# A group of small matmuls sooner, a transpose tied behind a feed-forward unit, four visits per chunk for six

## The chip, the cores and the metric

One core of a Trainium2 chip. The metric is the device time of one execution in microseconds (us). TensorE (PE in the rows) does matrix products, with its weight loads listed as PEld; VectorE is DVE, ScalarE is ACT, GpSimd is POOL, and SP only issues transfers. `L489` is line 489 of the kernel before.

## The reference

A delta-rule linear attention over 4 batches, 8 heads, 768 tokens and 48 channels a head, followed by two feed-forward layers of width 2048 on the 3072 x 384 result.

```python
k_n = k / (np.linalg.norm(k, axis=-1, keepdims=True) + 1e-06)
for t in range(S):
    y[:, :, t] = np.einsum('bhd,bhde->bhe', q[:, :, t], state)
    v_old = np.einsum('bhde,bhd->bhe', state, kt)
    state = state + bt[:, :, :, None] * np.einsum('bhd,bhe->bhde', kt, vt - v_old)
...
h = x @ w_in                     # layer 1: g = 0 below -1, h above 1, (h+1)^2/4 between
x = g @ w_out
h = x @ w_in; r = np.maximum(h, 0.0); out = (r * r) @ w_out      # layer 2
```

## The kernel before

**Attention** runs in 24 chunks of 32 tokens. A chunk c has six small steps on TensorE, each 64 little instructions but the last (`chunk_steps`): `ks` (keys times state; VectorE subtracts it from the values, L416), `tr` (the inverted triangle times that; ScalarE copies it out), `qs` (queries times state), `ku` (the state's update; VectorE and ScalarE copy the state to `st`, L456 and L457), `pu` (added onto the tile of `qs`; ScalarE copies it out) and `xt` (three transposes that make the chunk an input of the first layer). All but `ku` write PSUM tiles of one tag, `att`, which has two buffers; so do the grams.

**Triangles.** Chunks are taken in six groups of four. `gram(c)` (L272) multiplies a chunk's keys with its keys and queries, and VectorE masks the product into `gp` (L284). When a group's four grams are there, `tri` inverts its triangles together: VectorE transposes `gp` into `gm` (`begin`, L325), a short chain on ScalarE, VectorE and GpSimd scales it, then 30 steps follow, each a multiply and an add on GpSimd (L370, L376), one after another on the tile `tx`; last, VectorE transposes `tx` back into `gp` (`end`, L380). The `tr` of the group's first chunk needs that.

**Feed-forward.** A unit x is `hidden` of one block of tokens and one of 16 slices f of the width (nine matmuls into `h`, one buffer; then ScalarE L514 and L515 read it, VectorE L516, ScalarE L517, VectorE L518), then `rest` (ScalarE L526, VectorE L527: the high and the low part of g), and the output product `out_` of unit x - 2 (nine matmuls into `acc`). Layer 1 has nine blocks of 256 or 384 tokens (`SIZES` in chunks), layer 2 eight of 384. The block after the running one gets its attention meanwhile.

**Order.** TensorE's order is written by hand. Unit x has two slots, 2x and 2x+1; for each x the order is hidden(x), the small groups of slot 2x, out_(x-2), those of slot 2x+1. The tables `exa` (small matmuls) and `exb` (other work) hold what goes into which slot; `at[c]` is the slot of a chunk's first step, `ready[c]` that of its gram. The other engines' order is made at build time by a planner: it walks time by its own estimates of durations and puts on an engine's queue what it holds to be ready, what was traced earlier first. The engine then takes its queue strictly in that order. `tc.issue_after(ins)` lays an edge: what is traced inside, on the engine of `ins`, is queued behind `ins`. `later` does so for the last unit's L514 (ScalarE) and L516 (VectorE).

Group 1 is inverted around the start of the loop and its `end1()` is traced before the loop, with no edge. For groups 2 to 5 `tri_put` puts the scaling and the steps into the slots from `ready` on (all steps within six slots, `PACE`) and `end` into slot `at` of the group's first chunk, with no edge. The keys and queries of a chunk are loaded once, into a ring of six (`load_kq`); the chunk six further on is loaded when `qs` is done.

Of the kernel before, what the change touches and what calls it, by code (L numbers as in the profile page):

```python
# [21 lines left out]
GROUPS = [4] * 6  # L22
# [3 lines left out]
def kernel(  # L26
# [38 lines left out]
    LENT = 28  # L65
    RG = 3
    RAW = 3
    WT, WL = 3, 4
    GB = 2
    MANY = 4  # L70
# [31 lines left out]
    def att(shape, name):  # L102
        tag = "att"
        if turn[0] is not None:
            tag = early[turn[0] % len(early)]
            turn[0] += 1
        return ps.tile(shape, F32, tag=tag, bufs=2 if tag == "att" else 1, name=name)
# [6 lines left out]
    kqt, kvt, gp, nt, xh, xl = {}, {}, {}, {}, {}, {}  # L114


    def load_kq(c, tag="kqt", bufs=6):
        if c >= NCH:
            return
        t = kqt[c] = ring.tile([P, B2, H, 2 * T], F32, tag=tag, bufs=bufs, name="kqt")  # L120
        for o in range(2):
            nc.sync.dma_start(
                t[64 * o:64 * o + D].rearrange("p b h x -> p (b h x)"), kq[c, D * o:D * (o + 1)]
            )

    def load_kv(c):
        if c >= NCH:
# [87 lines left out]
    w2r = {}  # L215

    def fetch_w2(f):
        w2r[f] = ring.tile([P, 2, DM], F32, tag="kqt", bufs=6, name="w2r")
        nc.sync.dma_start(w2r[f], w2f[f])

    def place_w2(f):
# [33 lines left out]
    def per_bh(f):  # L255
        for h in range(H):
            for b in range(B):
                f(b, h, slice(T * b, T * (b + 1)), slice(64 * (b % 2), 64 * (b % 2) + D))

    def gram(c, lo=0, hi=2, late=0):  # L260


        n, j = group_of[c]
        if j == 0 and lo == 0:
            gp[n] = ring.tile([P, 2, GC, H, T], F32, tag="gp", bufs=2, name="gp")
            if GROUPS[n] < GC:
                nc.gpsimd.memset(gp[n][:, 0, GROUPS[n]:], 0.0)
        g = att([P, H, hi - lo, T], "g")

        def one_(b, h, p, pd):  # L270
            x = kqt[c][pd, b // 2, h]
            nc.tensor.matmul(  # L272
                g[p, h].rearrange("p x i -> p (x i)"), x[:, 0:T], x[:, lo * T:hi * T],
                start=h == 0, stop=True, skip_group_check=True,
            )

        per_bh(one_)

        dst = gp[n][:, lo:hi, j].rearrange("p x h i -> p h x i")
        if late > 1:  # L280
            nc.scalar.copy(dst, g)

        def keep():
            nc.vector.tensor_mul(  # L284
                dst,
                dst if late > 1 else g,
                mask[:, lo:hi].rearrange("p (o x) i -> p o x i", o=1)
                .to_broadcast([P, H, hi - lo, T]),
            )

        if late:
            return keep
        keep()
# [97 lines left out]
    def chunk_steps(c):  # L391
# [38 lines left out]
        def qs():  # L430
            o = t["o"] = att([P, H, D], "yy")
            of_state(o, 1)
            if c >= HEADS:
                kqt.pop(c)
                load_kq(c + 6)

        def pu():
            o = t["o"]
# [38 lines left out]
            nc.vector.tensor_sub(xl[n][:, :, cols], o, xh[n].bitcast(F32)[:, :, cols])  # L477
            done()

        return [ks, tr, qs, pu, ku, xt] if c < HEADS else [ks, tr, qs, ku, pu, xt]  # L480


    x2 = dram.tile([P, KT, NCH * P], F32, name="x2", bufs=1)
# [118 lines left out]
    w1f = flow(w1s)  # L602
    w1f.reverse()

    PACE = 6
    SPREAD = 3
    behind = [nullcontext]

# [6 lines left out]
    with tc.manual_schedule():  # L615
        for c in range(GC):
            load_kq(c)
        nc.sync.dma_start(bet, beta)
        first1()
        load_kq(4)  # L620
        load_kq(5)
        for c in range(3):
            load_kv(c)
        nc.gpsimd.memset(zero, 0.0)
        nc.gpsimd.memset(one, 1.0)
        nc.gpsimd.memset(tiny, 1e-36)
        nc.gpsimd.memset(neg1, -1.0)
        nc.scalar.activation(st[:, 0, 0, 0:1], one, AF.Sqrt, bias=zero)
        nc.gpsimd.memset(mask, 1.0)
        nc.gpsimd.memset(tx, 0.0)  # L630
        for b in range(B):
            for o, op in enumerate((ALU.is_ge, ALU.is_gt)):
                m_ = mask[T * b:T * (b + 1), o]
                nc.gpsimd.affine_select(
                    m_, m_, pattern=[[1, T]], compare_op=op, fill=0.0,
                    base=0, channel_multiplier=-1,
                )
        make_identity(nc, ident)
        for c in range(GROUPS[0]):
            gram(c, 0, 1)  # L640
        begin, pre, steps, end = tri(0, [(V, 0, 3), (V, 3, 9), (G, 9, T)])
        begin()
        go(pre[:1])
        masks = [gram(0, 1, 2, late=2)]
        cross_gram(0, 1)
        go(pre[1:])
        more_w1()
        masks += [gram(c, 1, 2, late=2) for c in range(1, GROUPS[0])]
        for c in range(HEADS):
            load_kq(c + 6)  # L650
        late = masks[HEADS:]
        masks[HEADS:] = [gram(c, late=1) for c in range(GFIRST[1], GFIRST[2])]
        go(steps)
        for c in range(3):
            value(c)
        ins = end()
        go(masks)
        behind[0] = lambda: tc.issue_after(ins.ins)
    ENGINES = {mybir.EngineType.PE}
    with tc.manual_schedule(engines=ENGINES):  # L660
# [15 lines left out]
        begin()  # L676
        go(pre)
        go(t1)
        end1()
        turn[0] = None  # L680

        SL = 2 * NF
# [2 lines left out]
        def put(n, slot, *fs):  # L685
            for i, f in enumerate(fs):
                exb.setdefault(SL * n + slot + i, []).append(f)

        def later(*fs):

            def one_(f):
                with tc.issue_after(marks[0].ins), tc.issue_after(marks[1].ins):
                    f()

            return [lambda f=f: one_(f) for f in fs]

        def put_a(n, slot, f):
            exa.setdefault(SL * n + slot, []).append(f)

        at, ready, due = {}, {}, [GFIRST[2]]
        for n in range(1, NB):
            todo = []
            for c in range(FIRST[n], FIRST[n] + SIZES[n]):
                left = {0: 1, 1: 1, 2: 0, 3: 2}[c % GC]
                for i, s_ in enumerate(chunk_steps(c)):
                    todo.append(((at, c) if i == 0 else None, s_))
                    x = due[0]
                    if i + left > 5 and x < NCH:  # L710
                        left -= 1
                        due[0] += 1
                        todo.append(((ready, x), lambda x=x: gram(x)))
            for i, (mark, s_) in enumerate(todo):
                o = 0 if n > 1 else HEAD
                slot = SL * (n - 1) + o + i * (SL - o) // len(todo)
                if mark:
                    mark[0][mark[1]] = slot
                put_a(0, slot, s_)
        for c in range(3, NCH):  # L720
            put(0, max(0, at[c] - 5), lambda c=c: value(c))

        def tri_put(g, a, z):
            begin, pre, steps, end = tri(g, [(G, 0, T)])
            begin()
            for i, s_ in enumerate(pre):
                put(0, a + i // 3, s_)
            a += 4
            for i, s_ in enumerate(steps):
                put(0, a + i * min(z - a, PACE) // len(steps), s_)  # L730
            put(0, z, end)

        for g in range(2, NG):
            a, z = ready[GFIRST[g] + GROUPS[g] - 1], at[GFIRST[g]]
# [99 lines left out]
```

## Time and profile before

| | us |
|---|---|
| median of 3 runs (1101.43 to 1104.24) | 1101.67 |
| the profiled execution | 1103.17 |
| its span, first to last instruction | 1101.1 |
| TensorE busy in the span | 995.3 (90%) |
| VectorE / ScalarE / GpSimd busy | 609.3 / 506.4 / 293.1 |
| mean granted TensorE clock | 0.963 of full speed |

A row of the timeline gives the start, the duration, the engine, the line, the operation, what it writes and reads, the shapes and the count; in brackets stands how long the engine was idle before it and what ended the idle time. TensorE's ends are modelled and overlap the next start, so that the time of a group of matmuls is best taken from its start to the start of the next.

### The profile page before, as it was taken

To read this page: it belongs to the slowest core of one execution; us is meant where nothing else is said; L and a number is where in the kernel's file an instruction comes from. 1 tells how busy PE (TensorE), PEld (TensorE's weight loads), DVE (VectorE), ACT (ScalarE), POOL (GpSimd) and SP (SyncE) were. 2 spreads that over 40 slices of the span, in tenths; PEclk is the share of its full clock that TensorE was granted. 3 is DMA by queue.
4 is the path that set the end of the run, shared out by engine and by line. 5 is a ranking of instruction groups with operands and counts; after the bars stand their busy time and mean duration, and the time that the engine had idled before them with its cause. 6 is when DMAs were issued, how large, how long until landed. Compare 5 with 4: busy or idle time off the path is not lost.

```text
span 1101.1 us, 32911 instructions
## 1 busy us (share of the span) xinstructions
PE 995.3 (90%) x14312; PEld 952.0 (86%) x14312; DVE 609.3 (55%) x1187; ACT 506.4 (46%) x1068; POOL 293.1 (27%) x446
## 2 busy tenths in 40 slices
PE   4345799969997997999799999899999999999998
PEld 3335699969986997899699999899999999999998
DVE  4998566754764583557644467744434343434333
ACT  1065466535544653555455666433333333333332
POOL 3467600850391058007600022310101010101000
PEclk9966899989998999899899999999999999999999
DMA  8065145223331340231211122201001010000000
GB/s 235 33 209 165 35 131 158 82 80 88 89 103 52 96 132 30 81 118 31 74 31 52 32 87 87 72 1 44 22 23 43 1 43 1 22 1 22 1 22 22
DMA packets 33488, 72.99 MB, mean 66 GB/s; under 512 B 3904, under 2 KB 17728, under 8 KB 33344
## 3 DMA queue, kind: packets, MB, share of 16 engines
q1 hardware_dynamic: 33344, 70.89, 20.9%
q8 instruction: 112, 1.84, 0.7%
q14 instruction: 32, 0.26, 0.1%
HBM read 55.15 MB, written 15.73 MB: 64 GB/s over the span
## 4 chain that ended last, share of the span: by engine, by line
PE 64%; POOL 15%; DVE 11%; issue 4%; ACT 3%; DMA 1%; SPq 0%; DVEq 0%; POOLq 0%; ACTq 0%
PE h L489 29%; PE acc L489 29%; POOL tx L376 7%; POOL t L370 7%; DVE g L518 1%; PE g L272 1%; DVE t L370 1%; DVE tx L376 1%; DVE wl L161 1%; PE tr L420 1%; PE yy L406 1%; DVE wl L164 1%; PE ks L406 1%; PE yy L440 1%; PE sps L451 1%
## 5 line engine op out<-in xcount | busy, mean ns | idle before, releaser
L489 PE MATMUL h<-xh,w 128*128 128x384 f32 (+1 forms) x1632 | 325.8, 336 | 31.3 <-ACT g L515 28.2
L489 PEld LDWEIGHTS h<-xh,w 128*128 128x128 f32 x1632 | 276.7, 193 | 37.5 <-ACT g L515 27.8
L527 DVE TENSOR_TENSOR gl<-g,gh 128x384 fp32r<-128x384 f32 (+1 forms) x272 | 167.2, 615 | 133.3 <-ACT gh L526 128.5
L526 ACT CAST gh<-g 128x384 fp32r<-128x384 f32 (+1 forms) x272 | 134.5, 494 | 209.7 <-DVE g L518 107.8
L489 PE MATMUL h<-xl,w 128*128 128x384 f32 (+1 forms) x816 | 181.3, 331 | 0.0
L489 PE MATMUL acc<-gh,w 128*128 128x384 f32 (+1 forms) x864 | 170.3, 333 | 7.2 <-ACT gh L526 6.5
L521 DVE TENSOR_TENSOR g<-r 128x384 f32<-128x384 f32 x128 | 71.3, 557 | 157.7 <-ACT r L520 157.7
L489 PE MATMUL acc<-w,gh 128*128 128x384 f32 x768 | 155.6, 337 | 1.6 <-DVE e L534 1.6
L520 ACT ACTIVATE r<-h,zero 128x384 f32<-128x384 f32 x128 | 74.5, 582 | 166.4 <-PE h L489 166.4
L489 PEld LDWEIGHTS acc<-gh,w 128*128 128x128 f32 x864 | 139.1, 193 | 12.7 <-ACT gh L526 6.6
L489 PEld LDWEIGHTS h<-xl,w 128*128 128x128 f32 x816 | 143.4, 193 | 0.0
L489 PEld LDWEIGHTS acc<-w,gh 128*128 128x128 f32 x768 | 136.3, 188 | 1.9 <-ACT gh L526 1.9
L514 ACT ACTIVATE r<-h,one 128x384 f32<-128x384 f32 (+1 forms) x144 | 78.4, 544 | 84.7 <-PE h L489 83.2
L518 DVE TENSOR_TENSOR g<-g,r 128x384 f32<-128x384 f32 (+1 forms) x144 | 89.0, 618 | 39.5 <-ACT r L517 38.2
L516 DVE TENSOR_SCALAR r<-r 128x384 f32<-128x384 f32 (+1 forms) x144 | 60.4, 419 | 84.9 <-ACT r L514 84.7
L376 POOL TENSOR_TENSOR tx<-tx,t 128x30 f32<-128x30 f32 (+16 forms) x171 | 95.5, 559 | 12.8
L370 POOL TENSOR_TENSOR t<-tx,gm 128x30 f32<-128x30 f32 (+16 forms) x171 | 92.7, 542 | 17.2 <-DVE tx L354 4.7
L489 PE MATMUL acc<-gl,w 128*128 128x384 f32 (+1 forms) x432 | 91.9, 322 | 2.3 <-DVE gl L527 2.3
L517 ACT ACTIVATE r<-r 128x384 f32<-128x384 f32 (+1 forms) x144 | 70.5, 490 | 49.5 <-DVE r L516 48.7
L249 POOL TENSOR_TENSOR kv<-kv,nt 128x384 f32<-128x384 f32 x24 | 21.7, 905 | 267.7 <-DMA kv<-in_kv_dram 73.2
L489 PE MATMUL acc<-w,gl 128*128 128x384 f32 x384 | 88.0, 337 | 0.0
L576 POOL CAST xh<-x2r 128x1152 fp32r<-128x1152 f32 x8 | 9.5, 1187 | 293.2 <-PE h L489 293.2
(85 smaller groups left out, 968.6 us busy)
## 6 DMA issues: line engine op xcount, KB each, us to landing
raw<-in_w_dram SPq DMA_DIRECT2D x64, 384.0 KB, 3.7
kqt<-in_kq_dram SPq DMA_DIRECT2D x48, 192.0 KB, 3.8
kv<-in_kv_dram SPq DMA_DIRECT2D x24, 384.0 KB, 3.1
w2f<-wl SPq DMA_DIRECT2D x32, 192.0 KB, 3.6
w2r<-w2f SPq DMA_DIRECT2D x16, 384.0 KB, 3.0
x2r<-x SPq DMA_DIRECT2D x8, 576.0 KB, 4.2
out_dram<-e SPq DMA_DIRECT2D x24, 192.0 KB, 1.9
x<-e SPq DMA_DIRECT2D x18, 192.0 KB, 3.4
```

The source lines that it names most:

```text
L370: eng.tensor_mul(t, x[:, lo:hi, j:j + 1].to_broadcast([P, hi - lo, w]), gm[:, j:j + 1, j + 1:T].to_broadcast([P, hi - lo, w]),)
L376: ins = eng.tensor_add(x[:, lo:hi, j + 1:T], x[:, lo:hi, j + 1:T], t)
L406: per_bh(lambda b, h, p, pd: nc.tensor.matmul(o[p, h], kqt[c][pd, b // 2, h, x * T:(x + 1) * T], st[pd, b // 2, h], start=h == 0, stop=x = ...
L489: nc.tensor.matmul(o, *((r, l) if swap else (l, r)), **flags)
L514: marks[0] = nc.scalar.activation(r, h, AF.Relu, bias=one)
L516: marks[1] = nc.vector.tensor_scalar(r, r, 2.0, 0.5, ALU.min, ALU.mult)
L517: nc.scalar.activation(r, r, AF.Square)
L518: nc.vector.tensor_add(g, g, r)
L520: marks[0] = nc.scalar.activation(r, h, AF.Relu, bias=zero)
L521: marks[1] = nc.vector.tensor_mul(g, r, r)
L526: nc.scalar.copy(ghi, g)
L527: nc.vector.tensor_sub(glo, g, ghi.bitcast(F32))
```

## The change

1. Where a chunk is past the first two, its steps are `ks`+`qs`, `tr`, `ku`+`pu`, `xt`: four groups, each in one slot.
2. A group's grams no longer have slots of their own. Those of the next group follow the third and the fourth step of the running group's first two chunks, in the same slot.
3. The grams read keys and queries from a ring of their own (`kqg`, two buffers, the chunk two further on loaded behind each gram); the main ring goes from six buffers to four and is loaded four chunks ahead. From chunk 4 on every chunk is loaded twice. The reloaded second-layer weights (`w2r`) use the main ring, four buffers for six.
4. The steps of an inversion are spread over the slots up to four before `at`, and begin one slot sooner behind the scaling.
5. `end` moves to slot `at` - 1 and `end1` to slot `at[4]` - 2, and both get `later`'s edge.

Worked out from the two programs, the slots are:

| group | last gram, before / after | `end`, before / after | first `tr`, before / after |
|---|---|---|---|
| 1 | ahead of the loop | ahead of the loop / 30 | 33 / 34 |
| 2 | 52 / 50 | 75 / 73 | 77 / 77 |
| 3 | 94 / 93 | 117 / 116 | 118 / 120 |
| 4 | 137 / 136 | 160 / 159 | 161 / 162 |
| 5 | 180 / 178 | 208 / 207 | 210 / 212 |

```diff
+    KQ, KG = 4, 2
...
-    def load_kq(c, tag="kqt", bufs=6):
-        if c >= NCH:
-            return
-        t = kqt[c] = ring.tile([P, B2, H, 2 * T], F32, tag=tag, bufs=bufs, name="kqt")
+    def load_kq(c):
+        if c < NCH:
+            kqt[c] = fetch_kq(c, "kqt", KQ)
+    kqg = {}
+    def load_kg(c):
+        if c < NCH and c not in kqg:
+            kqg[c] = fetch_kq(c, "kqg", KG)
...
-        w2r[f] = ring.tile([P, 2, DM], F32, tag="kqt", bufs=6, name="w2r")
+        w2r[f] = ring.tile([P, 2, DM], F32, tag="kqt", bufs=KQ, name="w2r")
...
+        src = kqt[c] if c < KQ else kqg[c]
-            x = kqt[c][pd, b // 2, h]
+            x = src[pd, b // 2, h]
         per_bh(one_)
+        if c >= KQ:
+            kqg.pop(c)
+            load_kg(c + KG)
...
-                load_kq(c + 6)
+                load_kq(c + KQ)
...
-        return [ks, tr, qs, pu, ku, xt] if c < HEADS else [ks, tr, qs, ku, pu, xt]
+        if c < HEADS:
+            return [ks, tr, qs, pu, ku, xt]
+        return [lambda: (ks(), qs()), tr, lambda: (ku(), pu()), xt]
...
-        load_kq(4)
-        load_kq(5)
+        for c in range(KG):
+            load_kg(KQ + c)
...
         go(t1)
-        end1()
...
-                left = {0: 1, 1: 1, 2: 0, 3: 2}[c % GC]
+                g, j = group_of[c]
+                due = []
+                if j < 2 and 1 <= g < NG - 1:
+                    m = GFIRST[g + 1]
+                    due = list(range(m + 2 * j, m + (2 * j + 2 if j == 0 else GROUPS[g + 1])))
                 for i, s_ in enumerate(chunk_steps(c)):
-                    todo.append(((at, c) if i == 0 else None, s_))
-                    x = due[0]
-                    if i + left > 5 and x < NCH:
-                        left -= 1
-                        due[0] += 1
-                        todo.append(((ready, x), lambda x=x: gram(x)))
+                    todo.append([((at, c) if i == 0 else None, s_)])
+                    if i > 1 and due:
+                        x = due.pop(0)
+                        todo[-1].append(((ready, x), lambda x=x: gram(x)))
...
+        put(0, at[GFIRST[1]] - 2, *later(end1))
...
-            a += 4
+            a += 3
             for i, s_ in enumerate(steps):
-                put(0, a + i * min(z - a, PACE) // len(steps), s_)
-            put(0, z, end)
+                put(0, a + i * (z - 4 - a) // len(steps), s_)
+            put(0, z - 1, *later(end))
```

## Rows read from the trace of the kernel before

**Rows 1.** The page, the span in 40 slices: TensorE's busy tenths, its granted clock

```profile
PE   4345799969997997999799999899999999999998
...
PEclk9966899989998999899899999999999999999999
```

**Rows 2.** Who waited for whom: us in total, times, longest us

```profile
PE h L489 <- ACT g L515: 28.2, 7, 8.4
...
DVE gp L380 <- POOL tx L376: 40.0, 5, 9.7
```

**Rows 3.** Timeline of TensorE: around the five long idle times, [idle before <-releaser]

```profile
131.20 1.65 PE L489 MATMUL h<-xh,w 128*128 128x256 f32 x6 [6.99 <-ACT g L515]
...
231.54 0.89 PE L406 MATMUL ks<-st,kqt 48*32 48x48 f32 x64
240.78 2.29 PE L489 MATMUL h<-xh,w 128*128 128x384 f32 x6 [8.36 <-ACT g L515]
...
243.83 1.40 PE L489 MATMUL acc<-gh,w 128*128 128x384 f32 x6
...
337.86 1.93 PE L272 MATMUL g<-kqt 48*32 48x64 f32 x64 [7.65 <-DVE gp L284]
...
442.40 1.93 PE L272 MATMUL g<-kqt 48*32 48x64 f32 x64 [7.69 <-DVE gp L284]
...
548.63 2.29 PE L489 MATMUL h<-xh,w 128*128 128x384 f32 x6 [6.43 <-ACT g L515]
```

**Rows 4.** Timeline of VectorE around the transpose back of group 2

```profile
228.86 0.54 DVE L477 TENSOR_TENSOR xl<-xt,xh 128x384 fp32r<-128x384 f32 x1
237.23 2.06 DVE L380 STREAM_TRANSPOSE gp<-tx 128x1024 f32<-128x1024 f32 x1 [7.83 <-POOL tx L376]
239.20 0.50 DVE L518 TENSOR_TENSOR g<-g,r 128x384 f32<-128x384 f32 x1
```

**Rows 5.** Timeline of VectorE: the transposes back of groups 3 and 4

```profile
334.71 2.01 DVE L380 STREAM_TRANSPOSE gp<-tx 128x1024 f32<-128x1024 f32 x1 [9.65 <-POOL tx L376]
...
439.29 2.04 DVE L380 STREAM_TRANSPOSE gp<-tx 128x1024 f32<-128x1024 f32 x1 [9.66 <-POOL tx L376]
```

**Rows 6.** Timeline of TensorE: the last grams of groups 2, 3 and 4

```profile
187.15 1.10 PE L272 MATMUL g<-kqt 48*32 48x64 f32 x64
...
283.38 1.10 PE L272 MATMUL g<-kqt 48*32 48x64 f32 x64
...
388.44 1.10 PE L272 MATMUL g<-kqt 48*32 48x64 f32 x64
```

**Rows 7.** Timeline of GpSimd: group 3's steps, instructions 1, 17 and 45 of 60

```profile
294.31 0.24 POOL L370 TENSOR_TENSOR t<-tx,gm 128x30 f32<-128x30 f32 x1 [0.63 <-DVE tx L354]
...
303.61 0.53 POOL L370 TENSOR_TENSOR t<-tx,gm 128x198 f32<-128x198 f32 x1
...
326.92 0.53 POOL L370 TENSOR_TENSOR t<-tx,gm 128x184 f32<-128x184 f32 x1
```

**Rows 8.** Timeline of TensorE: between small groups (first three rows), without them (last two)

```profile
263.86 0.88 PE L406 MATMUL ks<-st,kqt 48*32 48x48 f32 x64
...
268.81 1.31 PE L489 MATMUL h<-xh,w 128*128 128x384 f32 x6
...
270.57 0.88 PE L406 MATMUL yy<-st,kqt 48*32 48x48 f32 x64
...
705.73 1.21 PE L489 MATMUL acc<-w,gh 128*128 128x384 f32 x6
...
707.31 1.20 PE L489 MATMUL h<-xh,w 128*128 128x384 f32 x6
```

**Rows 9.** Timeline of TensorE: the first `tr` of chunks 0 and 2

```profile
48.47 1.50 PE L420 MATMUL tr<-kv,gp 32*32 32x48 f32 x64 [12.13 <-DVE gp L380]
...
106.65 0.88 PE L420 MATMUL tr<-kv,gp 32*32 32x48 f32 x64 [1.80 <-DVE kv L416]
```

**Rows 10.** DMA issues: count, KB each, median us to landing

```profile
kqt<-in_kq_dram SPq DMA_DIRECT2D x48, 192.0 KB, 3.8
```

More of the change, by code (lines that the diff above doesn't have):

```diff
@@ L114, with fetch_kq @@
     kqt, kvt, gp, nt, xh, xl = {}, {}, {}, {}, {}, {}
-    def load_kq(c, tag="kqt", bufs=6):
-        if c >= NCH:
-            return
-        t = kqt[c] = ring.tile([P, B2, H, 2 * T], F32, tag=tag, bufs=bufs, name="kqt")
+    def load_kq(c):
[5 more added lines that the diff above has]
+            kqg[c] = fetch_kq(c, "kqg", KG)
+    def fetch_kq(c, tag, bufs):
+        t = ring.tile([P, B2, H, 2 * T], F32, tag=tag, bufs=bufs, name="kqt")
         for o in range(2):
@@ L124, in load_kq @@
             )
+        return t
     def load_kv(c):
@@ L603 @@
     w1f.reverse()
-    PACE = 6
     SPREAD = 3
@@ L649 @@
         for c in range(HEADS):
-            load_kq(c + 6)
+            load_kq(c + KQ)
         late = masks[HEADS:]
@@ L698, in put_a @@
             exa.setdefault(SL * n + slot, []).append(f)
-        at, ready, due = {}, {}, [GFIRST[2]]
+        at, ready = {}, {}
         for n in range(1, NB):
@@ L705 @@
             for c in range(FIRST[n], FIRST[n] + SIZES[n]):
-                left = {0: 1, 1: 1, 2: 0, 3: 2}[c % GC]
-                for i, s_ in enumerate(chunk_steps(c)):
-                    todo.append(((at, c) if i == 0 else None, s_))
-                    x = due[0]
-                    if i + left > 5 and x < NCH:
-                        left -= 1
-                        due[0] += 1
-                        todo.append(((ready, x), lambda x=x: gram(x)))
-            for i, (mark, s_) in enumerate(todo):
+                g, j = group_of[c]
[3 more added lines that the diff above has]
+                    due = list(range(m + 2 * j, m + (2 * j + 2 if j == 0 else GROUPS[g + 1])))
+                for i, s_ in enumerate(chunk_steps(c)):
+                    todo.append([((at, c) if i == 0 else None, s_)])
+                    if i > 1 and due:
+                        x = due.pop(0)
+                        todo[-1].append(((ready, x), lambda x=x: gram(x)))
+                assert not due
+            for i, fs in enumerate(todo):
                 o = 0 if n > 1 else HEAD
                 slot = SL * (n - 1) + o + i * (SL - o) // len(todo)
-                if mark:
-                    mark[0][mark[1]] = slot
-                put_a(0, slot, s_)
+                for mark, s_ in fs:
+                    if mark:
+                        mark[0][mark[1]] = slot
+                    put_a(0, slot, s_)
+        put(0, at[GFIRST[1]] - 2, *later(end1))
         for c in range(3, NCH):
```

## The prediction

> **What bounds the kernel now.** The page's slices come first: from a tenth of the span on TensorE is nearly always busy, and full from three fifths on; in between stand single dips, and the granted clock dips with them [rows 1]. So time can be won in two ways: by closing the dips, or by giving TensorE less to do. The list of waits names what ends the dips: VectorE sits in front of the transpose back (L380) until GpSimd's last step (L376) is done, 40.0 us in five of the six times, and TensorE waits for ScalarE's second reader of `h` (L515), 28.2 us [rows 2]. The timelines join the two. Group 2: VectorE ends L477 at 229.4, then waits 7.83 us in the transpose, which stands in its queue ahead of L518 of unit 36, work that was ready long before [rows 4]. ScalarE waits for that L518 with its copy L526, behind which L515 of unit 37 is queued, and TensorE, which has `ks` of chunk 8 behind it at 231.54 and needs `h` for unit 38, starts again at 240.78 [rows 3]. In groups 3 and 4 VectorE is there even sooner and waits 9.65 and 9.66 us [rows 5]; there TensorE is held by a gram whose buffer VectorE should empty. The five idle times are 6.99 + 8.36 + 7.65 + 7.69 + 6.43 = 37.1 us [rows 3]. [...] **Together the dips cost 37.1 + 5 x 2.4 = 49 us.**
>
> The inversion itself is a chain. In group 3 the last gram starts at 283.38, the first step at 294.31 (10.9 us later), the transpose back at 334.71 (51.3 after the gram) [rows 5 to 7]; in groups 2 and 4 the transpose starts 50.1 and 50.9 us after the gram [rows 4 to 6]. With 2 us of transpose, `tr` may start some 53 us after the last gram, whatever the queues say. Two things then decide a dip: how much TensorE has to do between the gram and the point at which it runs dry, and how early the transpose stands in VectorE's queue. The planner put it there about 42 us after the gram, some 9 us before GpSimd was done: its estimate of the steps is too short.
>
> **The change, part by part.**
>
> *Visits.* A visit of TensorE to small matmuls costs more than these. A unit of nine matmuls takes 1.58 us among its like (705.73 to 707.31) and 1.76 us between two small groups (268.81 to 270.57) [rows 8]: about 0.19 us a visit. Chunks 2 to 23 lose two visits each, the 16 grams of the loop one each: 60 x 0.19 = 11 us. TensorE is the bound there, so it counts in full. If the little matmuls also followed each other faster inside a joined group it would be more, if the groups cost something at their seam it would be nothing; 0 to 15.
>
> *Group 1.* Its transpose goes to slot 30, behind L516 of unit 15. The idle time ended at unit 10 (131.20), so GpSimd was done by then; the 16 units from there to the gram at 187.15 (slot 52) take 3.5 us each [rows 3, 6], so the transpose comes 17 us later, and nobody waits for GpSimd. What is left is the 2 us of the transpose in front of one L518: 0.5 us.
>
> *Group 2.* The edge binds little here. Slot 73 belongs to unit 36, the very unit whose L518 was held up before; at the pace of the rows its L516 runs about 39 us after the gram, so the planner, which holds GpSimd done after 42, may put the transpose where it stood. Nor has TensorE more to do: between the last gram (slot 50 for 52) and `tr` of chunk 8 (slot 77) lie two narrow units more and one early `qs`, but two grams and six visits fewer. Before it would have been `ks` at 44.4 us after the gram [rows 3, 6], 0.8 for itself and two units of 1.66: 48.5; now about 48. `tr` waits for transpose and subtraction until 53: 5 us, with the clock 6.5. (If the transpose stands before L518 again, `h` runs dry at 45 and the dip is 8.8 + 1.5 as before; it may also hold L477, and with it a buffer that `qs` needs.)
>
> *Groups 3 and 4.* Here the edge binds: slots 116 and 159 mean units 58 and 79, whose L516 comes 48 and 47 us after the gram, so VectorE stands still for about 3 to 4 us and not 9.7. 27 and 26 slots lie between the gram and the point at which `h` runs dry (units 60 and 81). A slot took 2.17 us between `ks` at 263.86 (slot 85) and the gram at 283.38 (slot 94) [rows 6, 8]; without grams and with fewer visits I take 2.0 to 2.05. So TensorE runs dry 54 and 52.5 us after the gram. The transpose ends at 51.3 + 2 and 50.9 + 2, up to 0.5 later since the last gram now sits behind `xt`, and 0.8 later for the next reason; L518, L526 and L515 take 2 us more (239.20 to 240.78 and a little) [rows 3, 4]: 56.5 and 56. That leaves 3 and 4 us with some slow clock.
>
> The reason: the first 16 instructions of group 3's steps took 9.30 us (294.31 to 303.61) while VectorE worked, and the last 16, of the same sizes in reverse, 7.79 us (326.92 to 334.71) while it stood still from 325.06 on [rows 5, 7]. If VectorE works on, GpSimd's tail loses up to 1.5 us; half of that is in the sum, because VectorE still stands still for half of it.
> [...]
>
> *Group 5.* L516 of unit 103 comes 55 us after the gram, when GpSimd is done. Nothing is left.
>
> *Chunk 2's* `tr` moves from one unit behind `ks` to two; it waited 1.80 us for the subtraction, at half clock [rows 9]: 2 us won, 0 to 4.
>
> *At no cost.* The second copy of keys and queries adds 40 transfers of 192 KB that land in 3.8 us [rows 10]. A gram's load is issued behind the gram two before it, ten slots (17 us) ahead at the closest; cover for 13 us of hold-up in SP's queue, in which loads of raw weights and of values stand. At the start grams 6 and 7 now wait for a reload, at most two landings, 7.6 us, under the 12.13 us that TensorE sits idle before `tr` of chunk 0 [rows 9]. The weights' ring of four is still filled nine slots before use. Spreading the steps changes only how GpSimd's queue mixes them with the few products of `value`; they follow each other by their own chain. Behind the transpose, on VectorE, stand L518 and L527 of its unit, the next subtraction and the emptying of `att`: that is the 2 us above.
>
> *Sum.* Dips 49, left 0.5 + 6.5 + 3 + 4 + 0 = 14: 35 won. With 11 and 2: 48 us. The profiled execution took 1103.17 (span 1101.1), 1.5 above the median; 1103.17 - 48 = 1055, for the median **1054**.
>
> **The rivals.**
>
> *The transposes stay where they hurt.* L516 of the unit is only a lower bound, and the planner may again put the transpose before a reader that TensorE needs; or the chain starts later. Groups 2 to 4 then keep 8.36 + 7.65 + 7.69 + 3 x 2.4 = 31 us for the 13.5: 1071. For it speaks group 2, where the same unit is named; against it the 6 us later place in groups 3 and 4.
>
> *All dips close.* The scaling starts a little sooner or the planner queues the transpose later: 1054 - 14 = 1040.
>
> *Waits for the two `att` buffers.* `ks`+`qs` need both at once; a gram right behind `pu` needs one while `qs`'s is still being copied. Whether it gets the one that `tr` left is not to be seen in this trace. Eight grams follow `pu`; with 1 to 1.8 us each (the upper end the wait for an emptied tile in [rows 9]) about 10 us: 1064.
>
> *Slower: the reload.* If the load of `kqg` sits in SP's queue behind a transfer that waits for VectorE, all 16 grams stop TensorE, whose order is fixed, for a landing of 3.8 and 2.4 of slow clock: 16 x 6.2 = 99 us, 1153. It decides from 48 / 16 = 3 us a gram. Against it: 17 us of cover.
>
> **How the numbers follow.** Forecast 0.55, transposes staying 0.15, all closed 0.10, buffers 0.10, reload 0.06, and 0.04 for gains eaten up by several such waits to about nothing. The first four end between 1040 and 1071 and hold 0.90; with the bounds of the visits and of the other terms at the two ends the range is 1039 to 1075. About 0.3%, or 3 us, can be told from no change. Faster: 0.90; within: 0.03 of the last two cases; slower 0.07.
>
> **What would show it.** The wait of L380 for L376 falls from 40.0 to some 15 us and is longest in group 2; groups 1 and 5 have none. Idle times of TensorE over 5 us after the first 110 us are gone but for one. A unit between joined groups still takes 1.76 us, and there are 60 fewer of these pairs. From three fifths of the old span on nothing changes but the start time. It is wrong if TensorE waits before grams (for `kqg` or `g`) or before `yy`, or if L380 is reached earlier than L516 of the units named.

## The result and the profile after

| | us |
|---|---|
| median before, runs beside those of the changed kernel | 1101.72 |
| median after, 4 runs (1082.51 to 1085.58) | 1083.24 |
| ratio, 95% interval | 0.9831 [0.9810, 0.9852] |
| the profiled execution after, its span | 1082.51, 1080.8 |
| mean granted TensorE clock | 0.976 |

The change wins 18.5 us where 48 were forecast (1054, range 1039 to 1075). One execution of the kernel gram_tr below ran at a granted clock of 0.568 throughout (1612.6 us) and is left out of its numbers. In the changed kernel the `end` of an inversion, L380 before, is L395, and the step that it waits for, L376, is L391. The other lines: unit L507 with its readers L532 to L536 and L544, L545; grams L284, subtraction L431, `xl` L492, weight conversion L172 and L190, value products L260.

The slices of the page, after, which answer to [rows 1]:

```profile
PE   4445799979999999899999999999999999999998
...
PEclk9996999989999999899999999999999999999999
```

The list of waits, after, which answers to [rows 2] (who waited for whom: us in total, times, longest us):

```profile
PE h L507 <- ACT g L533: 17.6, 11, 4.0
...
DVE gp L395 <- POOL tx L391: 13.1, 3, 5.8
...
PE acc L507 <- DVE gl L545: 7.4, 2, 5.1
...
PE yy L421 <- DVE xl L492: 6.7, 1, 6.7
...
DVE wl L172 <- POOL w L190: 4.7, 2, 4.3
```

VectorE's wait in front of the transpose fell from 40.0 to 13.1 us, as forecast (15), and ScalarE holds `h` up for 17.6 us instead of 28.2. But the last three entries are new or larger (before, 2.3 us for the first of them, none for the second, 0.4 for the third). The timeline of VectorE shows where they begin: group 1's weight conversion, then the transposes back (they answer to [rows 4, 5]).

```profile
129.93 1.13 DVE L172 TENSOR_SCALAR wl<-raw 128x384 int32<-128x384 uint32 x1 [4.29 <-POOL w L190]
...
147.67 2.17 DVE L395 STREAM_TRANSPOSE gp<-tx 128x1024 f32<-128x1024 f32 x1
...
235.80 2.01 DVE L395 STREAM_TRANSPOSE gp<-tx 128x1024 f32<-128x1024 f32 x1 [5.80 <-POOL tx L391]
237.71 0.51 DVE L175 SCALAR_TENSOR_TENSOR wl<-wt,wl 128x384 int32<-128x384 int32 x1
238.14 0.55 DVE L492 TENSOR_TENSOR xl<-xt,xh 128x384 fp32r<-128x384 f32 x1
...
335.41 2.23 DVE L395 STREAM_TRANSPOSE gp<-tx 128x1024 f32<-128x1024 f32 x1 [2.07 <-POOL tx L391]
...
435.21 2.02 DVE L395 STREAM_TRANSPOSE gp<-tx 128x1024 f32<-128x1024 f32 x1 [5.24 <-POOL tx L391]
...
538.14 2.19 DVE L395 STREAM_TRANSPOSE gp<-tx 128x1024 f32<-128x1024 f32 x1
```

And the timeline of TensorE, its idle times over 1.2 us from 130 us on in the five groups, those put down to "issue", and one of 1.87 us between groups 1 and 2 (they answer to [rows 3]):

```profile
133.32 1.01 PE L507 MATMUL acc<-gl,w 128*128 128x256 f32 x3 [5.07 <-DVE gl L545]
...
160.62 1.48 PE L284 MATMUL g<-kqt 48*32 48x64 f32 x53 [1.55 <-issue]
...
198.54 1.65 PE L507 MATMUL h<-xh,w 128*128 128x256 f32 x6 [1.87 <-ACT g L533]
...
238.74 1.50 PE L421 MATMUL yy<-st,kqt 48*32 48x48 f32 x64 [6.67 <-DVE xl L492]
...
339.65 1.31 PE L507 MATMUL h<-xh,w 128*128 128x384 f32 x6 [1.46 <-ACT g L533]
...
375.86 0.43 PE L507 MATMUL h<-xh,w 128*128 128x384 f32 x1 [2.15 <-issue]
...
439.24 2.29 PE L507 MATMUL h<-xh,w 128*128 128x384 f32 x6 [4.05 <-ACT g L533]
...
477.09 0.42 PE L284 MATMUL g<-kqt 48*32 48x64 f32 x15 [1.28 <-issue]
```

To compare kernels I give each group of matmuls the time from its start to the next start, and take off what such a group takes undisturbed (a unit of nine 1.57 us, a narrow one 1.06, 0.1 more for each small neighbour, the small groups 0.25 to 1.03). What is left over is called **excess**: idle time and slow clock. From 84 us on, before had 70.2 us of it and after 62.3; visits and small groups fell by 11.6 and 1.5 us. So the visits are the forecast 11, and all the rest gave 7.9 us where the forecast had 35 for the dips and 2 for chunk 2's `tr`.

### The profile page after: what moved, and what is told of

Same layout as the page of the kernel before. It is cut to its first block, busy times and chain, and to the rows that moved or that the text cites. A ratio compares the mean times of both kernels' runs of the same rounds, so it can differ in the third digit from the quotient of the medians.

```text
span 1080.8 us, 33000 instructions
## 1 busy us (share of the span) xinstructions
PE 986.9 (91%) x14312; PEld 951.9 (88%) x14312; DVE 614.9 (57%) x1187; ACT 504.6 (47%) x1068; POOL 298.5 (28%) x446
## 4 chain that ended last, share of the span: by engine, by line
PE 67%; POOL 9%; DVE 5%; issue 3%; ACT 3%; DMA 0%; DVEq 0%; ACTq 0%; POOLq 0%; SPq 0%
PE acc L507 30%; PE h L507 30%; POOL tx L391 4%; POOL t L385 4%; PE g L284 1%; DVE g L536 1%; PE sps L466 1%; PE yy L455 1%; PE tr L435 1%; PE ks L421 1%; PE yy L421 1%; ACT r L532 1%; ACT g L533 1%; DVE gl L545 1%; DVE r L534 1%
## 5 line engine op out<-in xcount | busy, mean ns | idle before, releaser
L507 PE MATMUL h<-xh,w 128*128 128x384 f32 (+1 forms) x1632 | 322.0, 334 | 22.9 <-ACT g L533 17.6
L507 PEld LDWEIGHTS h<-xh,w 128*128 128x128 f32 x1632 | 276.6, 192 | 27.5 <-ACT g L533 19.2
L545 DVE TENSOR_TENSOR gl<-g,gh 128x384 fp32r<-128x384 f32 (+1 forms) x272 | 168.7, 620 | 141.7 <-ACT gh L544 135.6
L544 ACT CAST gh<-g 128x384 fp32r<-128x384 f32 (+1 forms) x272 | 134.5, 494 | 222.7 <-DVE g L536 107.8
L507 PE MATMUL h<-xl,w 128*128 128x384 f32 (+1 forms) x816 | 181.2, 331 | 0.0
L507 PE MATMUL acc<-gh,w 128*128 128x384 f32 (+1 forms) x864 | 168.1, 331 | 7.5 <-ACT gh L544 5.9
L507 PE MATMUL acc<-w,gh 128*128 128x384 f32 x768 | 155.5, 337 | 1.6 <-DVE e L552 1.6
L507 PEld LDWEIGHTS acc<-gh,w 128*128 128x128 f32 x864 | 139.3, 193 | 12.8 <-ACT gh L544 6.2
L507 PEld LDWEIGHTS h<-xl,w 128*128 128x128 f32 x816 | 143.1, 193 | 2.3 <-issue 2.3
L507 PEld LDWEIGHTS acc<-w,gh 128*128 128x128 f32 x768 | 136.3, 188 | 1.9 <-ACT gh L544 1.9
L532 ACT ACTIVATE r<-h,one 128x384 f32<-128x384 f32 (+1 forms) x144 | 78.2, 543 | 81.6 <-PE h L507 80.2
L536 DVE TENSOR_TENSOR g<-g,r 128x384 f32<-128x384 f32 (+1 forms) x144 | 87.9, 610 | 42.9 <-ACT r L535 41.8
L534 DVE TENSOR_SCALAR r<-r 128x384 f32<-128x384 f32 (+1 forms) x144 | 65.1, 452 | 69.8 <-ACT r L532 69.4
L391 POOL TENSOR_TENSOR tx<-tx,t 128x30 f32<-128x30 f32 (+16 forms) x171 | 98.8, 578 | 12.9
L385 POOL TENSOR_TENSOR t<-tx,gm 128x30 f32<-128x30 f32 (+16 forms) x171 | 95.2, 557 | 17.7 <-DVE tx L369 5.3
L507 PE MATMUL acc<-gl,w 128*128 128x384 f32 (+1 forms) x432 | 91.7, 321 | 7.4 <-DVE gl L545 7.4
L260 POOL TENSOR_TENSOR kv<-kv,nt 128x384 f32<-128x384 f32 x24 | 21.5, 898 | 245.3 <-ACT r L535 76.7
L507 PE MATMUL acc<-w,gl 128*128 128x384 f32 x384 | 88.0, 337 | 0.0
```

The lines of the kernel that those rows point to most:

```text
L385: eng.tensor_mul(t, x[:, lo:hi, j:j + 1].to_broadcast([P, hi - lo, w]), gm[:, j:j + 1, j + 1:T].to_broadcast([P, hi - lo, w]),)
L391: ins = eng.tensor_add(x[:, lo:hi, j + 1:T], x[:, lo:hi, j + 1:T], t)
L507: nc.tensor.matmul(o, *((r, l) if swap else (l, r)), **flags)
L532: marks[0] = nc.scalar.activation(r, h, AF.Relu, bias=one)
L534: marks[1] = nc.vector.tensor_scalar(r, r, 2.0, 0.5, ALU.min, ALU.mult)
L536: nc.vector.tensor_add(g, g, r)
```

## The experiments

The kernels that the argument compares, with the slots between a group's last gram and its first `tr` (worked out from the programs), and the excess by place. Stops are idle times put down to "issue", with the slow clock behind them.

| kernel | median us | ratio, 95% | slots, groups 2 to 5 | group 1 | groups 2 to 5 | stops |
|---|---|---|---|---|---|---|
| before | 1101.7 | | 25 24 24 30 | 8.8 | 40 | 0 |
| b_joined | 1109.19 | 1.0049 [1.0031, 1.0068] | 26 25 26 32 | 13.7 | 51 | 0 |
| b_end | 1074.48 | 0.9732 [0.9715, 0.9750] | 25 24 24 30 | 4.3 | 17 | 0 |
| b_both | 1062.63 | 0.9641 [0.9620, 0.9662] | 26 25 26 32 | 5.2 | 12.5 | 0 |
| after | 1083.24 | 0.9831 [0.9810, 0.9852] | 27 27 26 34 | 8.9 | 18 | 8.6 |
| grams_old | 1061.15 | 0.9615 [0.9599, 0.9631] | 26 25 26 32 | 7.7 | 14 | 0 |
| gram_own | 1085.24 | 0.9835 [0.9817, 0.9852] | 23 25 25 32 | 10 | 28 | 3 |
| end_late | 1070.74 | 0.9706 [0.9687, 0.9726] | 27 27 26 34 | 9 | 10 | 7 |
| six | 1098.83 | 0.9966 [0.9953, 0.9979] | 21 22 22 29 | 9.8 | 34 | <1 |
| six_quad | 1066.92 | 0.9674 [0.9659, 0.9688] | 29 29 35 37 | 6.5 | 6 | 0 |
| four_quad | 1055.64 | 0.9565 [0.9548, 0.9582] | 32 32 39 40 | 5.6 | 7 | 0 |
| four_quad_late | 1051.08 | 0.9529 [0.9514, 0.9544] | 32 32 39 40 | 5.8 | 2 | <2 |

### Parts of the change alone: b_end and b_joined

b_end, on the kernel before:

```diff
-        end1()
+        put(0, at[GFIRST[1]] - 2, *later(end1))
-            put(0, z, end)
+            put(0, z - 1, *later(end))
```

> The kernel before, with only the transpose back of groups 1 to 5 moved (behind a feed-forward unit, and one or two slots earlier); six groups of small matmuls and the grams as they were. Nothing is left out. Theory (what the earlier grams bring is that the inversion is over when L380 is issued; without them L380 still waits for GpSimd, and queued behind a unit it is only less in the way): the dips shrink from 50 us in all to 25 to 45, tr waits for L380 at several groups, 1085 to 1097 us. Rival (the queue place is all there is to it, and the earlier grams are not needed): the dips of groups 3 and 5 fall below 3 us and the sum to 28 us as in the changed kernel, 1081 us.

b_joined, on the kernel before:

```diff
-        return [ks, tr, qs, pu, ku, xt] if c < HEADS else [ks, tr, qs, ku, pu, xt]
+        return [lambda: (ks(), qs()), tr, lambda: (ku(), pu()), xt]
-                    if i + left > 5 and x < NCH:
+                    if i + left > 3 and x < NCH:
```

> The kernel before, with only a chunk's small matmuls in four groups instead of six (ks+qs, tr, ku+pu, xt), the grams still one group later, in slots of their own, and the transpose back where it was. Nothing is left out. Theory (visits cost TensorE 0.196 us each, and a joined ks+qs 0.13 us less; the dips of the groups come from VectorE's wait at L380 and don't change with it): 44 fewer visits, 8.6 us, and 22 x 0.13 = 2.9 us from ks+qs at the most: 1091 to 1095 us, the five dips of 9 to 11 us unchanged, no stop labelled 'issue' (no group holds more than 128 small matmuls). Rival (fewer groups leave TensorE less to do in VectorE's bad moments, and tr or ku wait): 1098 us or more.

Both expectations fell. The moved transpose alone wins 28.7 us (1074.48 against 1103.15), more than the whole change. The waits of b_end, and of b_joined (b_end has the line numbers of the kernel before; in b_joined the unit is L492, and its reader, L515 before, is L518):

```profile
PE tr L420 <- DVE kv L416: 16.9, 7, 7.6
...
DVE gp L380 <- POOL tx L376: 12.4, 3, 7.1
```

```profile
DVE gp L380 <- POOL tx L376: 53.2, 5, 14.5
PE h L492 <- ACT g L518: 51.9, 10, 13.9
```

For b_end both sides were half right: the early grams are not needed for most of the gain, but what is left does sit at `tr`, which waits behind the transpose (7.6 us in group 2). The four groups alone lose 6.0 us: their visits and joined groups give 11.3 us as expected (29.1 to 20.7 and 112.2 to 109.3), yet without the edge VectorE now stands 53.2 us before L380 instead of 40.0, and the excess grows by 17 us in sum. So the value of the four groups hangs on the transpose.

### Both parts together: b_both

Its edits are those of b_end and b_joined.

> The kernel before with two parts of the change, the four groups of b_joined and the moved transpose of b_end; grams one group later in slots of their own, one ring, steps within six slots. Nothing is left out. Theory A (four groups by themselves cost nothing: what they lost in b_joined was at the transposes, which stood ahead in VectorE's queue, and in the changed kernel it is the gram behind ku+pu and the new places of the grams): b_end's 1074.5 less 8.4 us for 43 visits and 2.9 us for ks+qs, 1062 to 1067 us. Theory B (joined groups bring VectorE's and ScalarE's work in bunches, and TensorE waits for it whatever the transposes do): 1072 us or more.

1062.63: theory A. With the transpose moved, four groups win 11.9 us over b_end (10.0 by the two ratios). The changed kernel has both parts and stands 20.6 us above this one; what it has besides is the second ring, the spread steps and the grams' new places.

### Which of the other parts eats the gain: one_load, pace6, grams_old

Each on the changed kernel; one_load:

```diff
-    KQ, KG = 4, 2
+    KQ, KG = 6, 2
-        src = kqt[c] if c < KQ else kqg[c]
+        src = kqt[c]
```

and without the reloads, with two more chunks loaded at the start; pace6:

```diff
-                put(0, a + i * (z - 4 - a) // len(steps), s_)
+                put(0, a + i * 6 // len(steps), s_)
```

grams_old has the rule of b_joined for the grams, in slots of their own.

> The changed kernel, with six buffers for keys and queries that grams and products share, so that no chunk is loaded twice (some 8 MB less from HBM, as in the kernel before). Nothing is left out. Theory (the stops labelled 'issue' come from the rate at which TensorE uses up its instructions, not from traffic): the three stops stay within 0.5 us each, at the same places of the instruction count, and the time is 1081 to 1085 us. Rival (the second loading slows the instruction transfers or others that TensorE waits for): the stops go or halve, 1074 to 1078 us.

> The changed kernel with the steps of an inversion in six slots instead of spread up to four slots before at. Nothing else is changed or left out. Theory (the steps follow each other by their own chain, so that the spread does nothing): 1081 to 1085 us. Rival (the spread steps are what eats the gain): 1062 to 1070 us.

> The changed kernel with the grams back where b_both has them (slots of their own, behind the last step of the first two chunks and the last two steps of the fourth); four groups, second ring, spread steps and moved transpose stay. Nothing is left out. Theory (it is the grams' places: behind ku+pu they bring the stops, 8.6 us, and their loads, masks and copies meet the other work of VectorE and ScalarE in the same slots): 1061 to 1066 us. Rival (it is the spread of the steps, whose place in GpSimd's and VectorE's queues holds up others): 1076 us or more.

1082.78, 1083.13 and 1061.15 us: the ring and the spread are worth nothing, as the prediction had it, and the grams' places cost 22 us. Of the 20.1 us of excess between the changed kernel and grams_old, 8.6 are the stops. The rest is spread: 3.6 us between 195 and 217 us, 2.6 in group 4, 1.5 in group 3, 1.2 in group 1 and several under 1 us. Why each of these comes with the grams' places was not tested. Group 2 keeps its dip in grams_old: there `yy` waits behind the transpose for a gram's mask (L299) in place of `xl`.

```profile
234.87 1.50 PE L421 MATMUL yy<-st,kqt 48*32 48x48 f32 x64 [6.48 <-DVE gp L299]
```

The distance to `tr` isn't what was lost here, since grams_old has one or two slots less of it. grams_old changes two things at once, the chunk and step that a gram follows, and its own slot in place of a shared one; no run separates them.

### The stops: gram_tr, gram_tr_look, gram_own

gram_tr, on the changed kernel (gram_own also gives the gram behind `tr` a slot of its own):

```diff
-                    if i > 1 and due:
+                    if i in (1, 3) and due:
```

> The changed kernel, with a chunk's grams behind its group tr and its group xt instead of behind ku+pu and xt. Nothing is left out. Theory (TensorE runs 192 short matmuls of ku, pu and a gram with their weight loads without a break, gets ahead of its own instruction stream, and stops): the three idle stretches that the changed kernel's trace labels 'issue' after 110 us (1.55, 2.15 and 1.28 us, with the slow clock behind them 8.6 us in all) are gone, none longer than 0.6 us is new, and the time is about 1075 us (1073 to 1077). Rival (the reloading of keys and queries crowds the transfers, and the place of the grams doesn't matter): the stops stay in number and size, 1082 to 1084 us. A second rival: a gram right behind tr delays ku and so the state of the next chunk; then the stops go and as much comes back as idle time before ks or ku, 1082 us or more.

> gram_tr again, for a trace at the usual clock. Nothing is left out. Theory: no stop labelled 'issue' behind ku+pu, but each of the eight grams behind tr waits some 0.7 us for ScalarE's copy of tr, with the slow clock behind it 8 to 12 us, 1085 to 1088 us. Rival: the grams wait for nothing, and the time is lost at the transposes back.

> The changed kernel, with the gram that stood behind ku+pu in a slot of its own between tr and ku+pu (eight such slots; the gram behind xt stays). Nothing is left out. Theory (192 short matmuls and their weight loads without a break outrun the instruction stream; and a gram directly behind tr, as in gram_tr, waits for the buffer that ScalarE's copy of tr frees): no stop labelled 'issue' over 0.6 us after 110 us, no gram that waits for ScalarE's copy, 8.6 us won less 8 x 0.2 us for the new visits: 1075 to 1078 us. Rival (gram_tr was slower than the changed kernel because a gram ahead of ku and pu delays the chunk's state, whatever it waits for): 1083 us or more.

gram_tr took 1085.8 to 1089.0 us (0.9856 [0.9837, 0.9875]), and gram_tr_look, a single execution, 1082.7; gram_own 1085.24 (ratio 0.9835 [0.9817, 0.9852]). In both the three stops of the changed kernel are gone, and in both something else took their place. In gram_tr each of eight grams waits for ScalarE's copy of `tr`. The list of waits of gram_tr_look, and one of the eight in its timeline of TensorE:

```profile
PE g L284 <- ACT kv L443: 9.3, 8, 1.2
```

```profile
246.54 1.10 PE L284 MATMUL g<-kqt 48*32 48x64 f32 x64 [1.24 <-ACT kv L443]
```

That is the `att` rival of the prediction at its true place: behind `tr`, not behind `pu`. In gram_own no gram waits, but the own slots leave 23, 25, 25 and 32 slots to `tr` where the changed kernel has 27, 27, 26 and 34; the excess of groups 2 to 5 rises from 18 to 28 us, and one stop of 1.72 us appears at another place. So removing the stops was right and didn't pay. That the loss comes from the shorter distance is argued, not shown: b_end, with 25, 24, 24 and 30 slots, has 17 us of excess there.

### Group 1: w_vec

```diff
-            (nc.vector if i else nc.gpsimd).tensor_sub(lo, box["t"], hi.bitcast(F32))
+            (nc.vector if i or f > 12 else nc.gpsimd).tensor_sub(lo, box["t"], hi.bitcast(F32))
```

> The changed kernel, with the subtraction for the low part of the last three weight tiles (L190, f 13 to 15) on VectorE instead of GpSimd. Nothing is left out. Theory (in group 1 the moved transpose no longer stands in VectorE's way, but L172 now waits 4.29 us there for a buffer that GpSimd frees only behind its inversion steps): that wait is gone, TensorE's idle stretches between 124 and 140 us (6.69 us in sum) fall below 2 us, the excess of that stretch falls from 8.9 to 1 or 2 us, and the time is about 1075 us (1074 to 1078). Rival (VectorE has no room there whatever it waits for, being short of time for the weights and the units both): the idle time moves to other reads of gl and h, 1081 to 1084 us.

1077.98 us (0.9778 [0.9763, 0.9792]), 5.3 won. GpSimd's timeline of the changed kernel has the inversion's last step, a value product, and only then the weights' low part that frees the buffer on which L172 waits.

```profile
127.90 0.26 POOL L391 TENSOR_TENSOR tx<-tx,t 128x30 f32<-128x30 f32 x1
128.12 0.83 POOL L260 TENSOR_TENSOR kv<-kv,nt 128x384 f32<-128x384 f32 x1
128.90 1.94 POOL L190 TENSOR_TENSOR w<-wl,w 128x384 fp32r<-128x384 f32 x2
```

The list of waits of w_vec has 0.4 us left of it:

```profile
DVE wl L172 <- POOL w L190: 0.4, 1, 0.4
```

The cause of L172's wait is shown; but the excess of the stretch falls from 8.9 to 5.8 us only, not to 2, since VectorE is then busy with weights and narrow units, with one pause of 0.53 us between 122 and 136 us, and TensorE waits for L533 (1.72 and 1.52 us). The other 2 us won are spread over other stretches. Each view was half right.

### Groups 2 and 4: end_late, and three together

```diff
-            put(0, z - 1, *later(end))
+            put(0, z + 1, *later(end))
```

> The changed kernel, with the transpose back of groups 2 to 5 placed two slots later (z + 1 instead of z - 1). Nothing is left out. Theory (in groups 2 and 4 the transpose back still stands on VectorE ahead of the xl and the gl that TensorE needs next, because the inversion ends some 9 us later than the place it was given): VectorE's idle time at L395 of 5.80 us (group 2) and 5.24 us (group 4) falls below 2 us in each, TensorE's idle stretches of 6.67 us at 238.74 and 4.05 us at 439.24 fall below 2 us, and the time is 1074 to 1078 us. Rival (tr of the group's first chunk needs the transposed inverse, and comes before it): TensorE then waits at tr for L395, as long as before or longer, 1082 to 1087 us.

1070.74 us (0.9706 [0.9687, 0.9726]), 12.5 won where 7 were expected. Group 2's idle time at L395 is not under 2 us but 3.55 in the timeline of VectorE, and the transpose stands ahead of the subtraction that `tr` waits for, no longer ahead of `xl`:

```profile
236.75 2.05 DVE L395 STREAM_TRANSPOSE gp<-tx 128x1024 f32<-128x1024 f32 x1 [3.55 <-POOL tx L391]
238.63 0.58 DVE L431 TENSOR_TENSOR kv<-kv,ks 128x384 f32<-128x384 f32 x1
...
239.53 0.62 DVE L536 TENSOR_TENSOR g<-g,r 128x384 f32<-128x384 f32 x1
```

An L536 still stands behind it, at 239.53, and TensorE waits another 1.20 us for `h` at 241.76. The timeline of TensorE has the two waits at `tr` that are left, one a group:

```profile
239.27 1.29 PE L435 MATMUL tr<-kv,gp 32*32 32x48 f32 x64 [2.84 <-DVE kv L431]
...
431.10 0.88 PE L435 MATMUL tr<-kv,gp 32*32 32x48 f32 x64 [1.45 <-DVE kv L431]
```

three is gram_own, w_vec and end_late in one kernel.

> The changed kernel with gram_own, w_vec and end_late together. Nothing is left out. Theory (the three causes are separate stretches of the run): the gains add, 1070.7 of end_late less 5 for the weights of group 1 less 5 for the stops that are left there (1.46, 1.58 and 1.20 us idle with the slow clock behind) plus 1.6 for eight visits: 1060 to 1064 us. Rival (one feeds on another: what one frees, VectorE's next stretch takes): over 1066 us.

1070.90 us (0.9703 [0.9678, 0.9727]): the gains don't add. What the other two win is lost again at `tr` (idle for 8.25 us in group 2, for 2.84 in end_late), where gram_own's slots bring it 23 slots behind the gram and not 27. The distance from gram to `tr` was the next thing to try.

### The distance: six, six_quad, four_quad, four_quad_late

six undoes the four groups in the changed kernel:

```diff
-        return [lambda: (ks(), qs()), tr, lambda: (ku(), pu()), xt]
+        return [ks, tr, qs, ku, pu, xt]
-                    if i > 1 and due:
+                    if i in (3, 5) and due:
+                        todo.append([])
```

The quad kernels put the four grams into the first chunk (j == 0) of the running group, and have w_vec's edit; four_quad_late has end_late's besides:

```diff
-                if j < 2 and 1 <= g < NG - 1:
+                if j == 0 and 1 <= g < NG - 1:
-                    due = list(range(m + 2 * j, m + (2 * j + 2 if j == 0 else GROUPS[g + 1])))
+                    due = list(range(m, m + GROUPS[g + 1]))
```

> The changed kernel with only its four groups undone: a chunk's small matmuls in six groups again, the grams in slots of their own (behind ku and xt of a group's first two chunks). Second ring, spread steps and the moved transpose stay. Nothing is left out. Theory now (the moved transpose is worth 28 us by itself, as b_end showed, and the four groups eat some 10 of it, by stops for instructions and by bringing VectorE sooner to the work on which it waits): 1070 to 1076 us, no stop labelled 'issue', the sum of the dips near b_end's 22 us. Rival (what eats it is the second ring, the spread steps or the grams' new places): 1080 us or more.

> six, with all four grams of the next group in the running group's first chunk (slots of their own behind tr, qs, ku and xt: 29, 29, 35 and 37 slots ahead of the first tr, where the kernel before has 25, 24, 24 and 30), and with the weights' change of w_vec. Nothing is left out. Theory (what is left of the dips of groups 2 to 4 in b_end, 17 us, is that the last gram stands too close to tr for the 52 us that scaling, steps and transpose take): VectorE's idle time at L395 is under 1 us in every group, tr waits for nothing, the dips of groups 2 to 5 fall to some 3 us, 1055 to 1061 us. Rival (VectorE's and GpSimd's queues hold the inversion up wherever its grams stand): the last gram is sooner and the end of the steps isn't, 1068 us or more.

> The changed kernel (four groups) with all four grams of the next group in the running group's first chunk (three in slots of their own behind ks+qs, tr and ku+pu, one behind xt: 32 to 40 slots ahead of tr) and the weights' change of w_vec. Nothing is left out. Theory A (four groups cost only through the inversion's lateness and the stops behind ku+pu+gram, and both are gone here): 8 us fewer visits and 3 us for joined ks+qs than six_quad, 1045 to 1052 us. Theory B (four groups cost something at each seam, whatever the inversion does): as six_quad or slower, 1057 us or more.

> four_quad with the transpose back of groups 2 to 5 two slots later (z + 1). Nothing is left out. Theory (group 2's steps end at 221.8 us, 4.10 us after VectorE has come to the transpose, which stands ahead of the xl on which the next chunk's yy waits; tr comes 11 us behind it and has room): the idle 3.85 us before yy goes, the excess of that stretch falls from 6.1 to about 1 us, 1050 to 1052 us. Rival (yy waits for something else there, or tr now waits for the transpose): 1055 us or more.

six came out on the rival's side (1080 us or more) and far beyond it, 1098.83: with 21 and 22 slots in front of `tr` TensorE waits there for the inversion in spite of the edge. The timeline of TensorE in group 2 (the page names no releaser; VectorE's L395 ended 0.1 us earlier, at 243.14):

```profile
243.24 1.50 PE L435 MATMUL tr<-kv,gp 32*32 32x48 f32 x64 [12.24 <-issue]
```

six_quad misses its range (1066.92 for 1055 to 1061), mostly through w_vec's remainder in group 1 (6.5) and group 2 (4.3 of excess, 3.0 us at L395); groups 3 to 5 are closed. four_quad is 11.3 us faster than it, which speaks for theory A, four groups without a cost at their seams, though 3.6 us above its range: group 2 again, where `yy` waits 3.85 us for `xl`. four_quad_late confirms that: the waits list is down to

```profile
DVE gp L395 <- POOL tx L391: 0.2, 1, 0.2
```

and the time is 1051.08 us. This version beats both kernels: 0.9529 of before, 32 us under the changed kernel.

## Why the prediction was wrong, point by point

**The grams' places: the step that failed.** The prediction took them for a gain (a slot or two sooner, a visit less each) and priced the danger at a wait for `att` behind `pu`, 10 us. The grams behind `pu` wait for no buffer. The new places cost 22 us (grams_old) all the same, 8.6 of it in stops of TensorE that no row of before shows. This step alone is three quarters of the miss of 29 us; the 6.3 us of the next paragraph make up nearly all of the rest. What made the other 13 of the 22 us stays open.

**The moved transposes: right mechanism, sized too high.** 35 us was the term; alone they brought 28.7 (b_end). By place, the changed kernel's dips compare with the forecast as follows:

- *Group 1* was to keep 0.5 us and kept 8.9, nothing won. The transpose did move back, by 21 us (126.19 to 147.67), and waited for nobody, but VectorE ran into the next thing that hung on the same GpSimd queue, L172 behind L190 behind the steps. The question "what is late next" was asked for VectorE's queue and not for GpSimd's.
- *Group 2* took the way given in brackets: the transpose stands ahead of `xl`, the `att` buffer is not free, `yy` idles 6.67 us, which the prediction had named as a sign of being wrong. That was priced at about 10 and measured 8.7, against 6.5 in the sum.
- *Group 3* 2.8 for 3, *group 5* 0 for 0: right. *Group 4* 6.4 for 4: the pause at L395 was 5.24 us for 3 to 4, because the transpose started 53.6 us after the last gram and not 50.9: the first step came 12.6 us after the gram for 11.4, and the steps took 41.0 us for 39.4.

**The slow clock of a dip:** no run shows, as a time of its own, the 2.4 us a dip that the sum and two of the rivals use. The trace of before shows a granted clock of 0.50 behind each of the five idle times, from TensorE's restart to 135.0, 244.1, 343.1, 448.9 and 554.8 us, that is for 3.8, 3.3, 5.2, 6.5 and 6.2 us. At a clock of 0.50 half of that is lost, 1.7 to 3.3 us a dip or 2.5 in the mean, an estimate from these times.

**Visits:** 11 us forecast; 11.6 measured in the changed kernel, and 1.5 in the small groups. The whole times of six_quad and four_quad differ by 11.3, those of b_end and b_both by 11.9. But b_joined shows what the prediction did not see: they were to be had only with the transposes out of the way.

**At no cost:** right for the ring (one_load) and the spread (pace6); the rival of the reload is out, since no gram of the loop waited for its load. **Chunk 2's `tr`:** 2 us forecast, 2.5 less excess up to 110 us. Its wait before was not at half clock: the granted clock was 1.00 from 104.9 to 107.6 us and 0.50 only behind that, from 107.8 to 111.0.

**The distance of 53 us** from last gram to `tr` was the right yardstick: the steps of groups 2 to 5 end 50 to 54 us after the last gram in every trace at the usual clock, and the transpose takes 2 more. I used it for 23 to 27 slots without asking what a few more would give. With the transpose at the same place, six has 34 us of excess in groups 2 to 5 at 21 to 29 slots and six_quad 6 at 29 to 37; the changed kernel has 18 and four_quad 7 at 32 and more. But it isn't the distance alone: end_late leaves it as it was, puts the transpose two slots later, and has 10 for 18.

## What to carry to other kernels

Price a moved step where it lands, not only where it leaves: the grams cost 22 us in their new places, for 16 visits that were worth 3. A queue edge that keeps a late result behind other work is worth much by itself (28.7 us here, and 12.5 for two slots more); what is left at it goes when the producer starts sooner, so that its whole chain (some 52 us here) fits in front of the consumer. Savings such as fewer visits can be lost again while such a wait is there. When one engine's wait is moved, look through the queue of the engine it waited for, since the next item there inherits the delay.

## What the runs showed of the hardware

**Stops of TensorE whole multiples of 256 records apart.** The three stops put down to "issue" come in or just behind a slot of `ku`, `pu` and a gram, 192 short matmuls with their weight loads: two of them 11 and 49 matmuls into the gram, one five matmuls into the unit that follows. Five more such slots run without one. Behind the first two the granted clock was 0.56 (160.6 to 163 us) and 0.53 (375.8 to 378), behind the third it stayed at 1.00. Counted over TensorE's records in the trace they come at numbers 5313, 14273 and 18114, that is 193, 193 and 194 beyond a multiple of 256, and within one of the same numbers in w_vec, end_late and one_load, whose times differ by up to 12 us. The other stops over 0.6 us that are put down to "issue" lie at 193 or 194 too: 1.72 us in gram_own, 1.64 in three and 0.60 to 0.95 in w_vec, end_late, one_load and pace6 at 5826, 0.64 in six at 6082, 0.66 and 0.86 in four_quad_late at 5314 and 8641. (The waits of six and three at `tr` are another thing: there the transpose ended just before.) The page's queues have, after:

```profile
q8 instruction: 112, 1.84, 0.7%
```

28,697 records / 112 packets are 256 a packet, 16.4 KB each, if all are TensorE's. Each stop had one such packet under way before it (158.17 to 159.05, 373.23 to 374.31, 474.91 to 475.84 us) and ended 1.25 to 1.57 us after that landed. This points to the instruction stream. It is not settled: other stretches of 256 records run through in 1.5 to 2.4 us without a stop, gram_tr's among them, and what makes the difference was not found. The three stops with such distances cost 8.6 us.

**GpSimd beside a working VectorE.** The steps of groups 2 to 5 took 39.0 to 40.4 us in the kernel before, where VectorE stood still up to 9.7 us of it, and 40.9 to 41.6 us in four_quad_late, where it stood still before the transpose for 0.2. The 60 instructions of a group alone took 33.7 to 34.8 us in sum before and 35.4 to 36.1 there, so that it isn't other work in GpSimd's queue; VectorE was busy for 20 to 26 us of the steps before and for 30 to 35 there. That is close to the 1.5 us that the prediction expected. That VectorE's work is the cause is inferred from these times, not shown.
